# Another token order, merged quarter tiles and an earlier input split in a fused attention and two-mixture kernel on one core

## The chip, the cores and the metric

One Trainium2 chip, one of its cores. The metric is the device time of one execution in microseconds, the median of the runs; the profile is of one further execution, whose own time is given beside its span.

## The reference

Attention with sigmoid weights, then two feed-forward blocks ("mixtures") on its output, all in fp32 at the surface:

```python
# q, k, v: (4, 12, 448, 64)
scores = scale * np.matmul(q, k.transpose(0, 1, 3, 2)) - np.log(S)
attn_out = np.matmul(1.0 / (1.0 + np.exp(-scores)), v)
x = attn_out.transpose(0, 2, 1, 3).reshape(B * S, H * D)       # (1792, 768)
h = x @ w_in;  x = (h * np.cos(h)) @ w_out                     # d_ff 2048
g = x @ w_gate; val = x @ w_val
out = (g * (1.0 / (1.0 + np.exp(-g))) * val) @ w_out2          # d_ff 1536
```

The weights come as 64-bit floats and are converted on the chip.

## The kernel before, in words

**Attention.** 24 pairs of heads, two per round of the loop in `attention` (L759 on). Each pair's q and k are split by VectorE into a rounded upper part and a rest (`split`, L771 and L772); TensorE makes the scores in three chunks of 128 keys from three products of parts (upper x upper, upper x rest, rest x upper; `scores`, L786), ScalarE takes the sigmoid of a chunk for both heads (`sigmoid`, L777), TensorE multiplies with v (`weigh`, L812, and `weigh_rest`, L821), and ScalarE copies the result out of PSUM into R (`leave`, L829). `beside` (L675) lets the planner lay other work between, in rounds that it takes for TWO_PAIRS (10.3) us long.

**Mixtures.** The tokens lie in two halves (h), each of 896 columns, and a unit is one half with two blocks of 128 hidden features; a stage is one mixture on one half. The first mixture has 16 units, 0 to 7 on the first half and 8 to 15 on the second; the second mixture has 12, 16 to 27. An up projection is done by a seven-product scheme (Strassen-Winograd): for each of the products 1 to 7 TensorE runs 9 matmuls of 448 columns (three inner blocks, three products of parts), L1093. The four results are the quarters 11, 12, 21 and 22 of the hidden matrix: the first digit is the feature block (i), the second the column half (j). A down projection of a unit is six down steps, each of 12 matmuls (L995); those of a unit run inside the next one. The order within a unit is a string of tokens (L293 to L296): a digit is an up product, "d" is a down step. `tokens` gives unit 0 and 1 the two strings in FIRST, later units of the first mixture ONE[c % 2] with c the number of the unit before within its stage (so unit 2 has ONE[1], unit 3 has ONE[0], and so on), units of the second mixture TWO twice (for the gate and the value), the last unit the two strings in LAST. Unit c of a stage does the column half j = c % 2 first in its down steps (`down_order`, L305): three steps for one half, then three for the other.

**PSUM.** Up products add in four banks a, b, d, e: 1 goes to a; `first_copy` takes a to b, and 2 adds to b (quarter 11); 6 adds to a; `second_copy` (L1027) takes a to e and 3 adds to e; 7 adds to a, 5 has d. `fifth`, `sum22` and `sum12` form quarters 22 and 12 in SBUF; 4 adds to a and gives 21. A token 2 or 6 waits for the first copy, 7 or 3 for the second, 4 for `sum22`. Down steps have two pairs of banks; `accumulate` (L937) takes a finished pair into R, and `banker` (L963) gives it to a later step, in some cases after a copy of earlier sums into it ("banks<-r").

**The path of a quarter.** In the first mixture `h_cos_h` (L905) does five steps on 448 columns (ScalarE `u`, VectorE `stt`, ScalarE sin, VectorE mult) and then `split_g` (L895): ScalarE rounds the result into the upper part of a g tile, VectorE writes the rest. In the second mixture ScalarE takes silu of the gate quarter and VectorE multiplies with the value's (`silu`, `silu_val`). There are six rooms for 448-column tiles (`tmps`) and four for g (`gslots`); a pair of g rooms comes free after the third and the sixth down step of a unit (L1008), and they go to the first that asked.

**Inputs.** x of a stage is split into upper part and rest for the seven products (`inputs`, L687, 1344 columns each, with subtractions before). The first half's are started when the last head of its second batch has left attention (L831), by `source`. X tiles for 7, 3 and 4 lie in memory that is lent to weight conversions until the end of attention: `lend_pool` (L423) runs four rooms of conversions, ENDS = ((18, 22),) stops new ones at pair 18 and takes the memory back at pair 22 (`swap`).

**Weights.** A converted tile goes back to DRAM and is loaded from there, combined for the scheme (L554), and split into upper part and rest (`operands`, L548; tiles wa, wb, x and s).

**The order of instructions.** Everything besides TensorE's list is ordered at build time by a planner (`Order`, `run` at L155): tasks offer a step with an engine, an assumed duration and a rank; the step that could start first goes next, and among those that could start together the one with the lowest rank. A rank is the time at which the result is due less a number in LEAD (L42), so a larger lead is a higher priority. Each engine then runs its list in that order.

Of the kernel before, what the change touches and what calls it, by code (L numbers as in the profile page):

```python
# [42 lines left out]
    "u": 2.09,  # L43
    "stt": 5.07,
    "sin": 6.46,
    "mult": 5.09,
    "ghi": 0.77,
    "glo": 8.31,
    "whi": 13.87,
    "wlo": 7.59,  # L50
    "c5": -11.35,
    "c7": 2.27,
    "c6": -1.57,
    "c3": -12,
    "xd": 4.42,
    "xhi": 11.87,
    "xlo": -11.87,
    "sv": -0.31,
    "acc": -11.58,
    "bank": -12,  # L60
    "first": -2.82,
    "second": -5.86,
    "fifth": 2.76,
    "s22": 35.5,
    "s12": -3.54,
    "silu": 14.75,
    "conv": 19.14,
    "by abs": 0.0,
    "by sum": 0.0,
    "by x": 0.0,  # L70
# [111 lines left out]
def block_kernel(  # L182
# [29 lines left out]
    def f32(ap):  # L212
        return ap.bitcast(F32)
# [60 lines left out]
    TWO_PAIRS = 10.3  # L274
    ENDS = ((18, 22),)
# [147 lines left out]
    def lend_pool(raw_qk):  # L423
# [9 lines left out]
        def swap():  # L433
            assert all(back.time is not None for back in backs)
# [25 lines left out]
    def conversions(raw=None, t=None, back=None, stop=None):  # L460
# [41 lines left out]
        if not ended:  # L502
            ended.append(True)
            free_t.give(room[:, :WT])
            free_t.give(room[:, WT:])
        else:
            for a in range(3):
                tmps.give(room[:, a * N:(a + 1) * N])
# [175 lines left out]
    source = [order.event() for _ in range(n_stages)]  # L684
    x_open = order.event()

    def inputs(s):  # L687
# [39 lines left out]
        yield source[s]  # L727
# [3 lines left out]
    def attention():  # L731
        with tc.tile_pool(name="at", bufs=2) as at:
# [52 lines left out]

            def scores(i):  # L786
                both = parts.pop(i)
                for c in range(NCH):
                    sc = score[i, c] = score_banks()
                    for n, (m, p) in enumerate(THREE):  # L790
                        for j, half in enumerate(heads):
                            nc.tensor.matmul(  # L792
                                sc[:, j], lhsT=both[half, m, S + c * P:S + (c + 1) * P], rhs=both[half, p, :S],
                                start=n == 0, stop=n == 2,
                            )
                    yield
# [54 lines left out]
            for i in range(0, NPAIR, 2):  # L851
# [25 lines left out]
                for stop, (last, after) in zip(stops, ENDS):  # L877
                    if i == last // 2 * 2:
                        stop[0].append(True)
                    if i == after // 2 * 2:  # L880
                        stop[1]()
            weigh(NPAIR - 1)
# [12 lines left out]
    def split_g(key, f, free):  # L895
        g = yield gslots
        n, _, j = key
        time = due["g", n, j]
        yield by(time - LEAD["ghi"], copy(0.6, g[:, 1], f))
        yield by(time - LEAD["glo"], vec(0.65, g[:, 0], f, f32(g[:, 1]), SUB))  # L900
        gs[key] = g
        g_ready[key].set()
        free()

    def h_cos_h(key, h, read):  # L905

        u = yield tmps
        time = due["g", key[0], key[2]]
        whole = u.bitcast(I32)
        yield by(time - LEAD["u"], act(0.55, out=whole, in_=h, func=AF.Copy, scale=INV2PI, bias=0.25))  # L910
        yield {"DVE": 0.66}, lambda _: nc.vector.scalar_tensor_tensor(
            out=u, in0=h, scalar=INV2PI, in1=whole, op0=ALU.mult, op1=ALU.subtract
        ), time - LEAD["stt"]
        yield by(time - LEAD["sin"], act(0.6, out=u, in_=u, func=AF.Sin, scale=2.0 * math.pi, bias=0.5 * math.pi))
        yield by(time - LEAD["mult"], vec(0.62, u, u, h, ALU.mult))
        read()
        yield from split_g(key, u, lambda: tmps.give(u))

    def silu(z, h, read, done, time):
# [297 lines left out]
```

## Time and profile before

| | us |
|---|---|
| median of 3 runs | 1064.78 (1064.68 to 1065.48) |
| profiled execution, its own time | 1063.94 |
| its span, first to last instruction | 1062.2 |
| TensorE busy (PE) | 1046.7 |
| VectorE busy (DVE) | 844.0 |
| ScalarE busy (ACT) | 628.2 |

The page has PE at 99% of the span, VectorE at 79%, ScalarE at 59%, GpSimd (POOL) at 15%. Times in the rows are us from the span's start unless marked ns. An idle time in brackets is that of the engine just before the row, with what released it. Matmul ends are modelled: one shows 0.36 us, while the next starts 0.2 us after it, so a printed idle time of PE is shorter than the delay of the starts. L258 and L261 are the helpers through which ScalarE's and VectorE's planned steps go, so tiles tell these apart. The first mixture begins at 136.5 us and ends near 575, the last matmul is at 1058.

### The profile page before, as it was taken

How to read it: one execution, taken by the hardware profiler on the slowest of the kernel's cores; microseconds unless marked ns; L12 is line 12 of the kernel's file. 1: busy time of each engine (PE TensorE's matmuls, PEld its weight loads, DVE VectorE, ACT ScalarE, POOL GpSimd, SP SyncE). 2: the span in 40 equal slices, each digit the busy share in tenths (PEclk: the TensorE clock that was granted, in tenths of full speed). 3: DMA queues.
4: the chain of work that ended last, by engine and by line, in shares of the span. 5: the costliest groups of instructions: out<-in, count | busy, mean ns of one | idle time of the engine just before them, and what ended most of it. 6: DMA issues, size and time to landing. Idle time of an engine off the chain costs nothing.

```text
span 1062.2 us, 14669 instructions
## 1 busy us (share of the span) xinstructions
PE 1046.7 (99%) x5459; PEld 914.0 (86%) x5459; DVE 844.0 (79%) x1116; ACT 628.2 (59%) x938; POOL 157.1 (15%) x139
## 2 busy tenths in 40 slices
PE   9999999999999999999999999999999999999998
PEld 4444479998988999999989999999999999999997
DVE  4779869998999988898899898888879744655644
ACT  5777766766778666676677656445444454433430
POOL 2120001112112201111021021111131110110100
PEclk9999999999999999999999999999999999999999
DMA  9997235656563245454422655554422412212002
GB/s 250 305 320 194 92 120 187 204 180 216 195 226 117 74 150 187 155 193 150 149 89 82 217 193 193 204 198 178 143 66 92 156 50 60 75 45 60 30 1 104
DMA packets 63047, 156.68 MB, mean 148 GB/s; under 512 B 9344, under 2 KB 35968, under 8 KB 62976
## 3 DMA queue, kind: packets, MB, share of 16 engines
q1 hardware_dynamic: 60096, 142.11, 41.9%
q0 software_dynamic: 2592, 13.17, 3.6%
q8 instruction: 43, 0.70, 0.3%
q10 hardware_dynamic: 288, 0.46, 0.2%
q14 instruction: 28, 0.23, 0.1%
HBM read 123.47 MB, written 32.24 MB: 147 GB/s over the span
## 4 chain that ended last, share of the span: by engine, by line
PE 89%; DVE 6%; ACT 3%; DMA 1%; issue 1%; SPq 0%; ACTq 0%; DVEq 0%
PE banks L1093 43%; PE banks L995 34%; PE banks L812 5%; PE banks L792 5%; DVE r L261 2%; DVE x L261 1%; PE banks L821 1%; PE banks L803 1%; ACT banks L258 1%; DMA raw<-in_w_in 1%; DVE u L261 0%; ACT x L700 0%; DMA rqk<-in_qk 0%; DVE wa L261 0%; DVE wb L261 0%
## 5 line engine op out<-in xcount | busy, mean ns | idle before, releaser
L1093 PE MATMUL banks<-x,wb 128*128 128x448 f32 x1044 | 224.6, 362 | 3.1 <-ACT banks L258 3.0
L995 PE MATMUL banks<-g,wb 128*128 128x448 f32 x1044 | 224.5, 362 | 0.7 <-DVE wb L261 0.5
L1093 PEld LDWEIGHTS banks<-x,wb 128*128 128x128 f32 x1044 | 195.3, 187 | 18.3 <-ACT banks L258 5.3
L1093 PE MATMUL banks<-x,wa 128*128 128x448 f32 x954 | 206.2, 363 | 3.0 <-ACT banks L258 2.5
L995 PEld LDWEIGHTS banks<-g,wb 128*128 128x128 f32 x1044 | 195.5, 187 | 14.6 <-DVE wb L261 0.9
L1093 PEld LDWEIGHTS banks<-x,wa 128*128 128x128 f32 x954 | 178.2, 187 | 18.3 <-ACT banks L258 4.4
L995 PE MATMUL banks<-g,x 128*128 128x448 f32 x540 | 115.7, 362 | 0.0
L261 DVE TENSOR_TENSOR r<-banks,r 128x896 f32<-128x896 f32 (+1 forms) x69 | 74.0, 1074 | 47.2 <-PE banks L995 46.9
L995 PEld LDWEIGHTS banks<-g,x 128*128 128x128 f32 x540 | 101.2, 187 | 6.8
L258 ACT ACTIVATE u<-u 128x448 f32<-128x448 f32 (+1 forms) x115 | 65.2, 574 | 65.5 <-DVE u L261 56.6
L261 DVE TENSOR_TENSOR u<-u,banks 128x448 f32<-128x448 f32 x117 | 72.0, 616 | 38.7 <-PE banks L1093 37.4
L258 ACT ACTIVATE g<-u 128x448 fp32r<-128x448 f32 x102 | 58.1, 574 | 69.3 <-DVE u L261 56.8
L995 PE MATMUL banks<-g,wa 128*128 128x448 f32 x432 | 92.4, 363 | 2.6 <-ACT banks L258 2.6
L777 ACT ACTIVATE a<-banks 128x896 f32<-128x896 f32 x84 | 75.0, 927 | 33.7 <-PE banks L792 28.7
L995 PEld LDWEIGHTS banks<-g,wa 128*128 128x128 f32 x432 | 80.8, 187 | 9.1 <-ACT banks L258 3.7
L261 DVE TENSOR_TENSOR wb<-t,wb 128x768 fp32r<-128x768 f32 x73 | 72.7, 1000 | 7.9 <-ACT wb L258 7.3
L1093 PE MATMUL banks<-x,s 128*128 128x448 f32 x360 | 78.5, 362 | 0.0
L554 POOL TENSOR_TENSOR sum<-t 128x384 f32<-128x384 f32 x21 | 26.3, 1251 | 339.6 <-DMA t<-swi 136.8
L258 ACT ACTIVATE banks<-banks 128x448 f32<-128x448 f32 x80 | 42.2, 528 | 56.5 <-PE banks L1093 53.8
L261 DVE TENSOR_TENSOR g<-u,g 128x448 fp32r<-128x448 f32 x102 | 66.5, 656 | 10.1 <-ACT g L258 10.1
L1093 PEld LDWEIGHTS banks<-x,s 128*128 128x128 f32 x360 | 67.5, 188 | 4.5
L258 ACT ACTIVATE r<-banks 128x896 f32<-128x896 f32 x52 | 47.6, 918 | 35.8 <-PE banks L995 35.8
(106 smaller groups left out, 1410.8 us busy)
## 6 DMA issues: line engine op xcount, KB each, us to landing
raw<-in_w_out SPq DMA_DIRECT2D x24, 768.0 KB, 4.8
t<-swi SPq DMA_DIRECT2D x32, 384.0 KB, 3.6
t<-swo SPq DMA_DIRECT2D x64, 192.0 KB, 2.9
rqk<-in_qk SPq DMA_DIRECT2D x46, 224.0 KB, 8.2
raw<-in_w_gate SPq DMA_DIRECT2D x12, 768.0 KB, 4.9
raw<-in_w_val SPq DMA_DIRECT2D x12, 768.0 KB, 5.8
t<-swd SPq DMA_DIRECT2D x44, 192.0 KB, 2.5
raw<-in_w_in SPq DMA_DIRECT2D x9, 768.0 KB, 4.7
```

Of the source, the lines that this page charges most:

```text
L258: return {"ACT": time}, lambda _: nc.scalar.activation(**kw)
L261: return {"DVE": time}, lambda _: nc.vector.tensor_tensor(out=out, in0=in0, in1=in1, op=op)
L554: on.tensor_tensor(out=out, in0=a, in1=b, op=op)
L777: nc.scalar.activation(out=a, in_=score.pop(key), func=AF.Sigmoid, bias=-math.log(S), scale=1.0 / math.sqrt(D))
L792: nc.tensor.matmul(sc[:, j], lhsT=both[half, m, S + c * P:S + (c + 1) * P], rhs=both[half, p, :S], start=n == 0, stop=n == 2,)
L803: nc.tensor.matmul(sc[rows, j], lhsT=raw[half, 1, REST:], rhs=raw[half, 0], start=True, stop=True)
L812: nc.tensor.matmul(banks[half, 6 + i % 2, :S], lhsT=vw[:, c, j], rhs=a[:, j], start=c == 0, stop=False, skip_group_check=True,)
L821: nc.tensor.matmul(banks[half, 6 + odd, :S], lhsT=last_v[rows, i // 2 % (2 * NS), j], rhs=a[rows, j], start=False, stop=True, skip_group_c ...
L995: nc.tensor.matmul(banks[:, first + e - d, :N], lhsT=w[:, m, e % KH, :], rhs=g[:, 1 - p], start=(i, m, p) == (0, 0, 0) and is_fresh and no ...
L1093: nc.tensor.matmul(bank, lhsT=w[:, m, k, :], rhs=x[p][:, k], start=(k, m, p) == (0, 0, 0) and i in (1, 5), stop=(k, m) == (KH - 1, 1), ski ...
```

## The change

Five things, cut to what matters:

- **Tokens.** FIRST[1], ONE[0] and LAST[1] are other strings with the same tokens.
- **First scores.** For the first pair of heads the upper x upper products of all three chunks are issued ahead of the other products.
- **Inputs of the first mixture.** Each of the seven x tiles waits for the quarter of R that it is made of (one batch, three head pairs), not for both batches. The lent rooms are taken back at pair 20 or, where their conversions are not through, at a later one. TWO_PAIRS is 10.9.
- **Two quarters as one tile.** `tmps` has three rooms of 2 x 448 columns and `gslots` two; quarters 12 and 22 go through `h_cos_h`, `silu`, `silu_val` and `split_g` as one tile of 896 columns after `sum12`, while 11 and 21 share a room and are handled one by one. A raw room that is given over at the end of the conversions yields one such tile instead of three single ones.
- **Leads.** Nearly all numbers in LEAD; three of them change assumed durations ("by abs" -0.26, "by sum" -0.08, "by x" +0.28: what the planner adds to VectorE's time for the absolute value of a weight, a weight sum, a cast of x).

```diff
-    "u": 2.09,      "stt": 5.07,    "sin": 6.46,    "mult": 5.09,   "ghi": 0.77,
-    "glo": 8.31,    "whi": 13.87,   "wlo": 7.59,    "xd": 4.42,     "xhi": 11.87,
-    "acc": -11.58,  "bank": -12,    "first": -2.82, "second": -5.86, "fifth": 2.76,
-    "by abs": 0.0,  "by sum": 0.0,  "by x": 0.0,
+    "u": -2.16,     "stt": 6.03,    "sin": 38.7,    "mult": 6.36,   "ghi": -11.5,
+    "glo": 5.57,    "whi": 11.53,   "wlo": 17.79,   "xd": -7.79,    "xhi": 8.43,
+    "acc": -9.4,    "bank": -7.95,  "first": -11.16, "second": 16.47, "fifth": 27.3,
+    "by abs": -0.26, "by sum": -0.08, "by x": 0.28,
...
-    TWO_PAIRS = 10.3
-    ENDS = ((18, 22),)
+    TWO_PAIRS = 10.9
+    ENDS = ((18, 20),)
...
-    FIRST = ('1652734', '1562d7d3dd4dd')
-    ONE = ('15267ddd3d4dd', '15d2d6d7d3d4d')
+    FIRST = ('1652734', '156d273ddd4dd')
+    ONE = ('1526d7dd3d4dd', '15d2d6d7d3d4d')
-    LAST = ('1526d734', '15d6273dddd4')
+    LAST = ('1526d734', '1d652d7d3dd4')
...
+            if s < NH:
+                yield left_attention[h, wanted[i]]
...
-        yield source[s]
+        wanted = {1: (0, 0), 2: (0, 1), 5: (1, 0), 7: (1, 1), 6: (1, 1), 4: (0, 1), 3: (1, 1)}
+        if s >= NH:
+            yield source[s]
...
+                for c in range(NCH if i == 0 else 0):
+                    product(both, banks[:, 2 * c:2 * c + 2, :S], c, 0)
                 for c in range(NCH):
                     sc = score[i, c] = score_banks()
+                    for n in range(1 if i == 0 else 0, 3):
+                        product(both, sc, c, n)
...
+                order.now = max(order.now, TWO_PAIRS * (i // 2 + 1) + 12.5)
-                if b % 2 and k == NP - 1:
-                    source[b // 2].set()
+                if k % KH == KH - 1:
+                    left_attention[b // 2, (b % 2, k // KH)].set()
...
-    def split_g(key, f, free):
-        g = yield gslots
+    def split_g(n, j, i, f, free):
+        both = i is None
+        if both:
+            g = yield gslots
+            halves["g", n, j] = [g, order.event(), 2]
+            part = g
+        else:
+            part = yield from half("g", (n, i, j), gslots)
+        hi, lo = (part[:, :, 1], part[:, :, 0]) if both else (part[:, 1], part[:, 0])
...
         def fifth():
-            keep["12"] = yield tmps
-            keep["22"] = yield tmps
+            two = keep["two"] = yield tmps
+            keep["12"], keep["22"] = two[:, 0], two[:, 1]
...
         def sum12():
-            yield from after("12", keep["12"], lambda: None)
+            two = keep["two"]
+            if layer == 1:
+                order.spawn(h_cos_h(n, 1, None, two, lambda: tmps.give(two)), 3)
...
-            for i in range(4):
-                gslots.give(mp.tile([P, 2, N], F32R, tag=f"g{i}", name=f"g{i}"))
-            for i in range(5):
-                tmps.give(mp.tile([P, N], F32, tag=f"u{i}", name=f"u{i}"))
+            for i in range(2):
+                gslots.give(mp.tile([P, 2, 2, N], F32R, tag=f"g{i}", name=f"g{i}"))
+            for i in range(2):
+                tmps.give(mp.tile([P, 2, N], F32, tag=f"u{i}", name=f"u{i}"))
```

## Rows read from the trace of the kernel before

**Rows 1.** The page's busy line of TensorE and its chain by engine.
```profile
PE 1046.7 (99%) x5459; PEld 914.0 (86%) x5459; DVE 844.0 (79%) x1116; ACT 628.2 (59%) x938; POOL 157.1 (15%) x139
...
PE 89%; DVE 6%; ACT 3%; DMA 1%; issue 1%; SPq 0%; ACTq 0%; DVEq 0%
```
**Rows 2.** Busy time by stretch: length, PE, PEld, DVE, ACT, POOL, clock, DMA.
```profile
260.00:360.00 100.00, 96.54 (x476) 88.46 (x476) 95.84 (x125) 76.89 (x115) 16.37 (x12) 1.00 0.51 172
...
562.80:790.00 227.20, 227.08 (x1134) 212.51 (x1135) 191.60 (x260) 121.78 (x186) 39.14 (x30) 1.00 0.51 170
```
**Rows 3.** Who waited for whom, PE alone: total us, times, longest.
```profile
PE banks L1093 <- ACT banks L258: 5.5, 9, 0.8
```
**Rows 4.** Timeline of PE in unit 3 (ONE[0]): start, length, work, idle before.
```profile
210.72 1.96 PE L1093 MATMUL banks<-x,x 128*128 128x448 f32 x9
213.30 2.08 PE L1093 MATMUL banks<-x,wb 128*128 128x448 f32 x9 [0.62 <-ACT banks L258]
```
**Rows 5.** Timeline of ScalarE at the same place.
```profile
212.72 0.53 ACT L258 ACTIVATE banks<-banks 128x448 f32<-128x448 f32 x1 [0.52 <-PE banks L1093]
```
**Rows 6.** Timelines of PE and VectorE in unit 5 (ONE[0]).
```profile
269.22 2.08 PE L1093 MATMUL banks<-x,wa 128*128 128x448 f32 x9 [0.62 <-ACT banks L258]
...
269.01 0.62 DVE L261 TENSOR_TENSOR g<-u,g 128x448 fp32r<-128x448 f32 x1
```
**Rows 7.** Timeline of PE at the first scores.
```profile
6.10 0.74 PE L792 MATMUL banks<-qk 64*128 64x448 f32 x2 [0.65 <-DVE qk L771]
7.16 5.17 PE L792 MATMUL banks<-qk 64*128 64x448 f32 x34 [0.32 <-DVE qk L772]
```
**Rows 8.** Groups by form: count, then busy us, mean ns, idle before.
```profile
L261 DVE TENSOR_TENSOR r<-banks,r 128x896 f32<-128x896 f32 x67 | 72.8, 1087 | 46.5 <-PE banks L995 46.3
...
L258 ACT ACTIVATE r<-banks 128x896 f32<-128x896 f32 x52 | 47.6, 918 | 35.8 <-PE banks L995 35.8
L258 ACT ACTIVATE u<-u 128x448 f32<-128x448 f32 x83 | 47.3, 574 | 47.3 <-DVE u L261 38.6 <-DVE u L911 8.5
...
L261 DVE TENSOR_TENSOR u<-u,u 128x448 f32<-128x448 f32 x48 | 30.4, 634 | 0.5 <-ACT u L258 0.4
```
**Rows 9.** Timelines of PE, ScalarE, VectorE: unit 4's start, then the tail.
```profile
233.21 1.96 PE L1093 MATMUL banks<-x,wb 128*128 128x448 f32 x9
...
234.90 0.62 DVE L261 TENSOR_TENSOR g<-u,g 128x448 fp32r<-128x448 f32 x1
...
236.31 0.62 DVE L261 TENSOR_TENSOR g<-u,g 128x448 fp32r<-128x448 f32 x1
...
1041.74 0.58 ACT L258 ACTIVATE g<-raw 128x448 fp32r<-128x448 f32 x1 [5.55 <-PE banks L995]
...
1042.35 0.62 DVE L261 TENSOR_TENSOR g<-raw,g 128x448 fp32r<-128x448 f32 x1 [3.72 <-ACT g L258]
...
1043.94 3.76 PE L995 MATMUL banks<-g,wb 128*128 128x448 f32 x18
```
**Rows 10.** Busy time of VectorE by stretch in attention: length, busy, clock, DMA.
```profile
20.00:40.00 20.00, 11.87 (x18) 1.00 1.06 296
...
80.00:100.00 20.00, 19.86 (x21) 1.00 0.70 185
```
**Rows 11.** Timeline of PE at other waits of the first mixture.
```profile
258.72 1.48 PE L995 MATMUL banks<-g,wa 128*128 128x448 f32 x6 [0.74 <-ACT banks L258]
...
298.52 0.68 PE L995 MATMUL banks<-g,wb 128*128 128x448 f32 x2 [0.22 <-ACT wb L258]
299.72 1.07 PE L995 MATMUL banks<-g,wb 128*128 128x448 f32 x4 [0.52 <-DVE wb L261]
...
344.85 1.48 PE L995 MATMUL banks<-g,wa 128*128 128x448 f32 x6 [1.48 <-ACT banks L258]
```
**Rows 12.** ScalarE in attention (timeline), then its casts of x (groups).
```profile
18.68 0.92 ACT L777 ACTIVATE a<-banks 128x896 f32<-128x896 f32 x1 [0.40 <-PE banks L812]
...
L700 ACT ACTIVATE x<-r 128x1344 fp32r<-128x1344 f32 x20 | 26.5, 1324 | 10.7 <-PE banks L1093 6.2 <-DVE r L261 4.4
```

More of the change, by code (lines that the diff above doesn't have):

```diff
@@ L42 @@
 LEAD = {
[L43 to L66, printed above, removed]
+    "u": -2.16,
+    "stt": 6.03,
+    "sin": 38.7,
+    "mult": 6.36,
+    "ghi": -11.5,
+    "glo": 5.57,
+    "whi": 11.53,
+    "wlo": 17.79,
+    "c5": -11.17,
+    "c7": -1.62,
+    "c6": -12,
+    "c3": -2.55,
+    "xd": -7.79,
+    "xhi": 8.43,
+    "xlo": -12,
+    "sv": 6.71,
+    "acc": -9.4,
+    "bank": -7.95,
+    "first": -11.16,
+    "second": 16.47,
+    "fifth": 27.3,
+    "s22": 17.01,
+    "s12": 2.09,
+    "silu": 40.74,
     "conv": 19.14,
-    "by abs": 0.0,
-    "by sum": 0.0,
-    "by x": 0.0,
+    "by abs": -0.26,
+    "by sum": -0.08,
+    "by x": 0.28,
 }
@@ L433, in swap @@
         def swap():
-            assert all(back.time is not None for back in backs)
+            if any(back.time is None for back in backs):
+                return
+            backs.append(order.event())
             pool.__exit__(None, None, None)
@@ L506, in conversions @@
         else:
-            for a in range(3):
-                tmps.give(room[:, a * N:(a + 1) * N])
+            tmps.give(room[:, :2 * N].rearrange("p (i t) -> p i t", i=2))
     def landed(event, t=None):
@@ L879, in attention @@
                         stop[0].append(True)
[L880 removed]
+                    if i >= after // 2 * 2:
                         stop[1]()
+            assert x_open.time is not None
             weigh(NPAIR - 1)
@@ L893, in block_kernel @@
     gs = {}
-    def split_g(key, f, free):
-        g = yield gslots
-        n, _, j = key
-        time = due["g", n, j]
[L899 to L902, printed above, removed]
-        free()
[L905 to L911, printed above, removed]
+    halves = {}
@@ new lines, in half, with give_half @@
+    def half(kind, key, slots):
+        n, i, j = key
+        if (kind, n, j) not in halves:
+            halves[kind, n, j] = [None, order.event(), 2]
+            halves[kind, n, j][0] = yield slots
+            halves[kind, n, j][1].set()
+        yield halves[kind, n, j][1]
+        return halves[kind, n, j][0][:, i]
+    def give_half(kind, key, slots):
+        n, _, j = key
+        entry = halves[kind, n, j]
+        entry[2] -= 1
+        if not entry[2]:
+            slots.give(halves.pop((kind, n, j))[0])
@@ new lines, in split_g @@
+    def split_g(n, j, i, f, free):
[7 more added lines that the diff above has]
+        hi, lo = (part[:, :, 1], part[:, :, 0]) if both else (part[:, 1], part[:, 0])
+        time = due["g", n, j]
+        yield by(time - LEAD["ghi"], copy(0.92 if both else 0.6, hi, f))
+        yield by(time - LEAD["glo"], vec(1.1 if both else 0.65, lo, f, f32(hi), SUB))
+        for e in range(2) if both else (i,):
+            gs[n, e, j] = g[:, e] if both else part
+            g_ready[n, e, j].set()
+        free()
@@ L912, in h_cos_h @@
+    def h_cos_h(n, j, i, h, read):
+        both = i is None
+        u = (yield tmps) if both else (yield from half("u", (n, i, j), tmps))
+        time = due["g", n, j]
+        whole, wide = u.bitcast(I32), 0.37 if both else 0.0
+        yield by(time - LEAD["u"], act(0.55 + wide, out=whole, in_=h, func=AF.Copy, scale=INV2PI, bias=0.25))
+        yield {"DVE": 0.66 + 1.3 * wide}, lambda _: nc.vector.scalar_tensor_tensor(
             out=u, in0=h, scalar=INV2PI, in1=whole, op0=ALU.mult, op1=ALU.subtract
@@ L919, in silu, with silu_val @@
-    def silu(z, h, read, done, time):
-        yield by(time, act(0.6, out=z, in_=h, func=AF.Silu))
+        yield from split_g(n, j, i, u, lambda: tmps.give(u) if both else give_half("u", (n, i, j), tmps))
+    def silu(z, h, read, done, time, wide=0.0):
+        yield by(time, act(0.6 + wide, out=z, in_=h, func=AF.Silu))
         read()
         done.set()
-    def silu_val(key, z, z_done, h, read, free, time):
+    def silu_val(n, j, i, z, z_done, h, read, free, time):
         yield z_done
-        yield by(min(time, due["g", key[0], key[2]] - LEAD["sv"]), vec(0.62, z, z, h, ALU.mult))
+        yield by(min(time, due["g", n, j] - LEAD["sv"]), vec(0.62 if i is not None else 1.1, z, z, h, ALU.mult))
```

60 lines of the change are left out of this document (33 added, 27 removed).

## Prediction

> **What bounds the kernel now.** I read the page's busy line and its chain first. TensorE is busy 1046.7 us and carries 89% of the chain that ended last [rows 1]. The kernel ends when TensorE has gone through its list, so time is won only where TensorE stands still; the reader should look for gaps on PE. The table by stretch says where they lie: 3.46 us of 100 in 260 to 360 us, 0.12 of 227.2 in 562.8 to 790 us [rows 2]. The second mixture hardly waits, the first does. The list of PE's waits says for what: 5.5 us in 9 waits of up products (L1093) for a ScalarE copy that reads and writes PSUM [rows 3].
>
> The PE timeline shows what one such wait costs. The up product at 210.72 has 9 matmuls 0.2 us apart, so the next could begin at 212.52. It begins at 213.30: 0.78 us, and about 0.11 more while the pipeline fills again: 0.89 us are lost where the row prints an idle time of 0.62 [rows 4]. So I add 0.27 to a printed idle time. The copy that it waits for starts at 212.72, when the product has drained, and lasts 0.53 us [rows 5]. This is token 7 right behind token 6: `second_copy` must take bank a to bank e before 7 adds to a.
>
> **The change part by part.**
>
> *Token order.* ONE[0] has "67" side by side before and "6d7" after. Units 3, 5, 7, 9, 11, 13 and 15 run ONE[0], so there are seven such waits; the row at 213.30 stands for them. A down step is 12 matmuls, 2.4 us, against a copy of 0.53 us and hand-offs of about 0.2: well covered. Removed: 7 x 0.89 = **6.2 us**. What is late next is the down step that is pulled ahead: it starts 0.89 + 1.8 = 2.7 us sooner and needs its half's g tiles by then. In the unit whose token 7 started at 269.22 VectorE wrote one g tile from 269.01 for 0.62 us, until 269.63 [rows 6]; the down step came 1.91 us after token 7's start and would now start 2.7 us before that, at 268.4. So 1.2 us are short in that unit if the order stays. The list is made anew with the nearer due time and this g tile stood behind work that is due later, so I take 0; bounds 0 and 1.2, and rival (b) is the case in which it is the rule.
>
> *The first scores.* TensorE does two matmuls at 6.10 and then waits for the lower part of the split until 7.16 [rows 7]. With the first product of all three chunks ahead, six matmuls stand in this hole. The 34 that follow take 5.17 us [rows 7], 0.30 us for the two of a pair of heads. Two pairs move: 0.6 us at most, 0 if the sigmoids set the pace. I take **0.5 us**, nearer the upper end, since TensorE's row starts on its own split and no sigmoid becomes later.
>
> *Two quarters as one tile.* An ACTIVATE of 448 columns lasts 574 ns, one of 896 lasts 918; VectorE's tensor_tensor 634 and 1087 ns [rows 8]. Merging two saves 230 ns on ScalarE and 180 ns on VectorE; a unit of the first mixture has three of each, 0.7 and 0.5 us of 27. VectorE is busy 95.84 of 100 us in 260 to 360 us [rows 2], so this is relief where it is short, but not on TensorE's path: it counts under the waits below.
>
> *What the merged tile costs.* The second pair's room for g is free only when the last down step of the unit before is through. The conversion is then one ScalarE pass of 0.92 and one VectorE pass of 1.09 us [rows 8], both ahead of the first matmul; with hand-offs, 2.2 to 2.3 us. Two places have little room.
> At the end LAST[1] now has "3dd4": one up product, 1.8 us, stands between that down step and the first of the closing six. Before, this late conversion starts at 1041.74 and ends at 1042.97, and the closing six start unhindered at 1043.94 [rows 9]. Merged, it starts when the step has drained, 1042.3, and ends near 1044.4: **+0.6 us** with the refill; bounds 0.3 and 0.9.
> In the units with an odd number the next one starts with "15d", 3.6 us of room, seven places (units 1 to 13). In the one that began at 233.21, behind unit 3, VectorE ended the two late conversions at 235.52 and 236.93 [rows 9], 2.3 and 3.7 us after. A single pass needs about 1.4 of that, so the first one queued 0.9 us. A merged one with this queueing is through at 3.2 of 3.6 us. I take 0.15 each, **+1.0 us**; bounds 0 and, with the second one's queueing of 2.3 us, 1.1 each, 7.7 us.
>
> The Trainium skill, Perfetto Trace Analysis, section Optimizing Scalar/DVE Operations, speaks against merging here: where these two engines are not saturated but hold up another, breaking instructions up may end the work sooner. VectorE's rows at the tail are idle for the most part, so by that rule single tiles would leave the 0.6 us out and the sum would be 1056.4; no run here shows both forms.
>
> *Inputs split as their heads leave, rooms given back, TWO_PAIRS.* Before, the first stage's x tiles wait for the last head of the second batch, and VectorE is then full, 19.86 of 20 us in 80 to 100 us, while it had 11.87 of 20 in 20 to 40 us [rows 10]. What moves is casts and subtractions into that idle time, and what it frees is time for two to four more weight conversions in attention. Cover: TensorE's own work in attention hides both engines. If it fails by the planner's longer round (10.9 against 10.3 us), a full VectorE slips by at most 0.2 us in each of some nine rounds, 2 us; a ScalarE that gets the casts is rival (c). I take 0, since VectorE's idle time in 20 to 40 us is the nearest row.
>
> *The other waits of the first mixture.* The largest are at 258.72, 298.52, 299.72 and 344.85 [rows 11]: with 0.27 each, 1.01 + 0.49 + 0.79 + 1.75 = 4.0 us. The two near 299 wait for weights that ScalarE and VectorE split late; with earlier conversions and less VectorE work they go: -1.3. The other two wait for a down bank that `banker` fills with earlier sums, behind the same full engines; the new leads reorder them, and between all gone and as much again (-2.8 to +2.8) I take half gone, by the relief above: -1.4. Together **-2.7 us**.
>
> **Sum.** The profiled run's own time is 1063.94 us: its span of 1062.2 and 1.74 around it. The median of the runs, 1064.78, is 0.84 above; the sum is put on the median. -6.2 - 0.5 + 0.6 + 1.0 - 2.7 = -7.8: **1057.0 us**.
>
> **The rivals.**
> (a) *Only the token order counts.* The other waits move but stay: -6.2 - 0.5 + 0.6 + 1.0 = -5.1, **1059.7 us**. For it: a lead decides only among steps that are ready at the same time. Against: VectorE gets less work in a stretch that is 96% full.
> (b) *The wait moves.* The down step waits for g where 7 waited for its copy, so the 6.2 us stay: -0.5 + 0.6 + 1.0 - 2.7 = -1.6, **1063.2 us**. For it: 269.63 against 268.4 [rows 6]. Against: that needs 0.9 us in all seven units, and VectorE only has to take that one pass earlier.
> (c) *Slower: casts of x on ScalarE among the sigmoids.* The lead "by x" makes the planner count a cast on VectorE 0.28 us dearer, and a longer round leaves a start on ScalarE open in it. A cast lasts 1.32 us there; between sigmoids ScalarE had idle times of 0.40 us [rows 12], and TensorE waits for sigmoids in each half round. It decides from a cast that is queued ahead of a sigmoid in a gap shorter than 1.32 us. Seven casts that hide nothing cost 9.2 us: -5.1 + 9.2 = +4.1, **1068.9 us** with the other waits staying. For it: the four hand-over gaps are short. Against: the q/k scores run ahead by three chunks, and before the change VectorE took these casts.
> (d) *The room for g comes too late* in all seven units, 7.7 in place of 1.0: -2.7 other waits kept: -7.8 + 6.7 = -1.1, **1063.7 us**. Against: the 2.3 us of queueing belong to a second pass behind a first, and the merged tile has only one.
> That the first scores gain nothing is 0.5 us on any of these.
>
> **How the numbers follow.** Forecast 0.50 (1053 to 1058.3); (a) 0.27 (1058.3 to 1062); (b) below its full price 0.06 (1062 to 1062.6), so faster 0.83; (b) and (d) near their price, 0.09, are within 0.2%, which is about what a measurement of this kernel can tell from no change (2.1 us); (c) and its like 0.08, slower. Low end: all four other waits gone, first scores at 0.6, no new wait but the tail's 0.6: -6.2 - 0.6 - 4.0 + 0.6 = -10.2, 1054.6; the two waits that the list counts beside the seven [rows 3] (5.5 - 7 x 0.62 = 1.2 us printed, 1.7 with 0.27 each) may give up to 2 more: 1052.5. High end 1062.5, which leaves (b), (d) and (c) out, 0.17.
>
> **What would show it.** Right: tokens 6, d, 7 without a gap and PE's waits on L1093 for ScalarE copies down from 9 to about 2; no PE gap near 6.8 us; ScalarE and VectorE rows of u and g with 896 columns; x tiles from about 30 us on; more loads of `lr` than before; a gap of half a microsecond ahead of the last 72 matmuls. Wrong: PE waiting for g ahead of the first down step of a unit; new waits in attention; the waits for weights near 299 us still there, which would mean that the earlier x split bought no conversion.

## The result: 0.84% faster

| | us | before, beside it | ratio, 95% interval |
|---|---|---|---|
| before | 1064.78 | | |
| after | 1055.61 (1053.94 to 1058.6, 4 runs) | 1064.73 | 0.9916 [0.989, 0.9942] |
| after, profiled execution | 1054.24, span 1052.4 | 1063.94, span 1062.2 | |

The forecast was 1057.0 in a range of 1052.5 to 1062.5. The profiled executions differ by 9.7 us, in their own times as in their spans. Where that came from can be counted on TensorE. From the first up product on I added up by how much each matmul starts later than 0.2 us after the one before it; this is called **lost** below. The time from the first score to the first up product is called the length of **attention**. The end is counted from 0.2 us behind the start of the last matmul.

| us | before | after | difference |
|---|---|---|---|
| lost in the mixtures | 14.65 | 4.12 | -10.53 |
| attention | 130.38 | 131.34 | +0.96 |
| from the last matmul to the end | 3.82 | 3.69 | -0.13 |
| sum | | | -9.70 |

So the mixtures gave more than the whole, and attention took a tenth of it back.

The page of after, its busy line and its chain by engine, beside [rows 1]; then the table by stretch, beside [rows 2]:

```profile
PE 1043.5 (99%) x5459; PEld 914.9 (87%) x5459; DVE 839.9 (80%) x1049; ACT 618.3 (59%) x866; POOL 154.7 (15%) x140
...
PE 95%; DMA 2%; POOL 1%; DVE 1%; ACT 0%; issue 0%; POOLq 0%; ACTq 0%; DVEq 0%; SPq 0%
```
```profile
260.00:360.00 100.00, 100.00 (x502) 93.75 (x501) 91.96 (x108) 72.44 (x101) 21.01 (x15) 1.00 0.42 138
```

In that stretch TensorE's idle 3.46 us are gone and VectorE is busy 4 us less. Who waited for whom, PE alone, whole span (total us, times, longest), beside [rows 3]:

```profile
PE banks L815 <- ACT a L783: 1.5, 2, 0.9
...
PE banks L1038 <- DVE r L261: 1.0, 1, 1.0
PE banks L1141 <- ACT banks L258: 0.7, 1, 0.7
...
PE banks L1038 <- DVE g L261: 0.2, 1, 0.2
```

Of the nine waits of up products (L1141, before L1093) for a ScalarE copy one is left. It stands in unit 0 in both kernels. The largest wait is new and lies in attention: L815, scores that wait for a sigmoid. (Before, the list has one wait of TensorE for a sigmoid, of 0.2 us.) The place of [rows 4 and 5] in unit 3, PE and then ScalarE:

```profile
210.95 1.96 PE L1141 MATMUL banks<-x,x 128*128 128x448 f32 x9
212.75 2.56 PE L1038 MATMUL banks<-g,wa 128*128 128x448 f32 x12
215.15 1.96 PE L1141 MATMUL banks<-x,wb 128*128 128x448 f32 x9
...
212.95 0.53 ACT L258 ACTIVATE banks<-banks 128x448 f32<-128x448 f32 x1 [0.72 <-PE banks L1141]
```

Token 6, the down step and token 7 follow each other to the hundredth (1.8 and 2.4 us), and the copy, 212.95 to 213.48, lies under the down step.

### The profile page after: what moved, and what is told of

It is laid out like the page before. It is cut to its first block, busy times and chain, and to the rows that moved or that the text cites. A ratio compares the mean times of both kernels' runs of the same rounds, so it can differ in the third digit from the quotient of the medians.

```text
span 1052.4 us, 14528 instructions
## 1 busy us (share of the span) xinstructions
PE 1043.5 (99%) x5459; PEld 914.9 (87%) x5459; DVE 839.9 (80%) x1049; ACT 618.3 (59%) x866; POOL 154.7 (15%) x140
## 4 chain that ended last, share of the span: by engine, by line
PE 95%; DMA 2%; POOL 1%; DVE 1%; ACT 0%; issue 0%; POOLq 0%; ACTq 0%; DVEq 0%; SPq 0%
PE banks L1141 47%; PE banks L1038 38%; PE banks L824 5%; PE banks L795 4%; DMA vs<-in_v 1%; PE banks L815 1%; PE banks L833 1%; DMA t<-swi 1%; POOL cv L555 1%; DMA rqk<-in_qk 0%; DVE wa L261 0%; ACT g L258 0%; DVE r L261 0%; POOL sum L555 0%; DVE g L261 0%
## 5 line engine op out<-in xcount | busy, mean ns | idle before, releaser
L1141 PE MATMUL banks<-x,wb 128*128 128x448 f32 x1044 | 224.1, 362 | 0.0
L1141 PEld LDWEIGHTS banks<-x,wb 128*128 128x128 f32 x1044 | 195.8, 188 | 13.0
L1141 PE MATMUL banks<-x,wa 128*128 128x448 f32 x954 | 205.8, 362 | 0.9 <-ACT banks L258 0.7
L1141 PEld LDWEIGHTS banks<-x,wa 128*128 128x128 f32 x954 | 178.6, 187 | 14.6 <-ACT banks L258 1.5
L261 DVE TENSOR_TENSOR u<-u,banks 128x448 f32<-128x448 f32 x124 | 76.2, 616 | 62.2 <-PE banks L1141 60.0
L258 ACT ACTIVATE wb<-t 128x768 fp32r<-128x768 f32 x75 | 62.9, 838 | 50.5 <-PE banks L1141 34.0
L555 POOL TENSOR_TENSOR sum<-t 128x384 f32<-128x384 f32 x26 | 35.3, 1358 | 344.5 <-DMA t<-swi 121.3
L1141 PE MATMUL banks<-x,s 128*128 128x448 f32 x360 | 78.5, 362 | 0.0
L261 DVE TENSOR_TENSOR g<-u,g 128x448 fp32r<-128x448 f32 (+1 forms) x78 | 68.8, 890 | 11.4 <-ACT g L258 11.1
L258 ACT ACTIVATE wa<-t 128x768 fp32r<-128x768 f32 x61 | 51.0, 840 | 40.8 <-PE banks L1141 18.0
L258 ACT ACTIVATE g<-u 128x448 fp32r<-128x448 f32 (+1 forms) x78 | 54.0, 699 | 35.4 <-PE banks L1038 18.8
```

The costliest lines, as they stand in the source:

```text
L258: return {"ACT": time}, lambda _: nc.scalar.activation(**kw)
L261: return {"DVE": time}, lambda _: nc.vector.tensor_tensor(out=out, in0=in0, in1=in1, op=op)
L555: on.tensor_tensor(out=out, in0=a, in1=b, op=op)
L1141: nc.tensor.matmul(bank, lhsT=w[:, m, k, :], rhs=x[p][:, k], start=(k, m, p) == (0, 0, 0) and i in (1, 5), stop=(k, m) == (KH - 1, 1), ski ...
```

## The experiments

Each kernel was timed, and profiled once; its ratio is to runs of the kernel before beside it, whose medians were 1064.47 to 1065.59 us. "Lost" and attention are those of the one profiled execution.

| | edit | us (low to high) | ratio to before | lost in mixtures | attention | `lr` loads |
|---|---|---|---|---|---|---|
| before | | 1064.78 | | 14.65 | 130.38 | 11 |
| after | | 1055.61 (1053.94 to 1058.6) | 0.9916 [0.989, 0.9942] | 4.12 | 131.34 | 14 |
| e1 | before with the new ONE[0] | 1080.97 (1079.95 to 1085.59) | 1.0151 [1.012, 1.0182] | 28.77 | 132.31 | 11 |
| e2 | after with the old ONE[0] | 1063.74 (1061.56 to 1066.26) | 0.9978 [0.9965, 0.999] | 12.36 | 130.82 | 14 |
| e3 | after with the old input split | 1076.65 (1073.01 to 1079.73) | 1.0095 [1.0066, 1.0124] | 19.70 | 138.44 | 12 |
| e4 | after with the old first scores | 1053.52 (1053.24 to 1053.96) | 0.988 [0.9863, 0.9897] | 4.04 | 130.51 | 14 |
| e5 | after, unchanged | 1054.38 (1053.02 to 1054.97) | 0.9889 [0.987, 0.9908] | 4.16 | 130.18 | 14 |
| e6 | after with single tiles | 1063.42 (1061.0 to 1066.93) | 0.9978 [0.9964, 0.9992] | 11.76 | 133.86 | 14 |
| e7 | after with the old leads | 1064.8 (1063.47 to 1068.87) | 0.9999 [0.9983, 1.0014] | 14.92 | 130.25 | 14 |
| e8 | after, landings assumed later | 1059.59 (1059.09 to 1061.26) | 0.9942 [0.9923, 0.996] | 4.05 | 136.24 | 14 |
| e9 | after, loads from 78 us on | 1055.23 (1054.3 to 1056.08) | 0.9902 [0.9882, 0.9921] | 4.07 | 131.61 | 14 |
| e10 | after, leads rounded | 1055.24 (1054.38 to 1056.13) | 0.9899 [0.9877, 0.9921] | 4.07 | 133.16 | 14 |
| e11 | before, leads rounded | 1068.91 (1066.74 to 1071.91) | 1.0031 [1.0015, 1.0047] | 17.82 | 132.36 | 11 |
| e12 | e8 and e9 together | 1053.25 (1052.73 to 1053.61) | 0.9895 [0.9879, 0.9912] | 4.09 | 130.20 | 14 |

Two of the sums hold a second thing besides waits: 4.4 us of e1's 28.77 and 1.6 us of e7's 14.92 were lost by matmuls that ran at a lower clock behind a wait. That is told below.

### The token string, alone and taken back (e1, e2)

```diff
-    ONE = ('15267ddd3d4dd', '15d2d6d7d3d4d')
+    ONE = ('1526d7dd3d4dd', '15d2d6d7d3d4d')
```

> The kernel before with one string changed: ONE[0] is '1526d7dd3d4dd'. Theory (the token order hides the copy): the seven waits of 0.89 us ahead of token 7 go, 6.2 us, time 1058.5 us; PE's waits of L1093 for ScalarE copies fall from 9 to 2. Rival (the wait moves): the down step that is pulled ahead waits for its g tile, PE's waits for g or for weights grow by as much, time 1063 to 1065 us.

e2 is this diff turned round, in the kernel after.

> The changed kernel with ONE[0] as before. Theory: seven waits of 0.89 us come back, 6.2 us more, 1061.8 us. Rival (in the new schedule other things bound the first mixture): less than 3 us more, under 1058.5 us.

In e1 the seven waits of token 7 are gone, as the step says, and the kernel is 1.5% **slower**, far outside both the theory and its rival. Four lines of PE's waits in e1, then two places of its timeline, in unit 5's down step and in unit 8, and the table by stretch right behind the second:

```profile
PE banks L1093 <- DVE x L261: 4.7, 2, 3.6
PE banks L995 <- ACT banks L258: 3.3, 2, 2.3
PE banks L1093 <- DVE u L261: 3.1, 2, 2.7
PE banks L995 <- ACT wb L258: 2.9, 2, 1.5
...
303.77 0.67 PE L995 MATMUL banks<-g,wb 128*128 128x448 f32 x2 [1.50 <-ACT wb L258]
...
363.75 2.61 PE L1093 MATMUL banks<-x,wb 128*128 128x448 f32 x6 [3.59 <-DVE x L261]
...
363.39:366.80 3.41, 3.04 (x8) 2.75 (x9) 3.41 (x4) 0.00 (x0) 1.42 (x1) 0.50 0.56 190
```

TensorE now waits for weights, x tiles, bank copies and quarters that the two other engines made in time before. VectorE is busy 96 of 100 us in the first mixture [rows 2], and with another string the planner makes another list throughout: 6.4 us went and 20.6 came. Of the 20.6, waits are 16.2. The other 4.4 were lost behind them: in three stretches (305.36 to 308.78, 363.39 to 366.80 and 820.78 to 824.19 us) the granted clock of TensorE was 0.50, the lower of its two levels (1.2 of 2.4 GHz), and matmuls started 0.37 us apart in place of 0.20. In each case TensorE had stood still shortly before, for 1.50 and 1.31, 3.59, and 2.70 us. In e2 the same seven waits come back with the old string:

```profile
PE banks L1141 <- ACT banks L258: 5.2, 8, 0.8
```

(eight with the one in unit 0), and 8.24 us are lost more than in after. So the string ONE[0] decides those seven waits in either kernel, but what it is worth depends on what it stands beside: -8.2 us lost in the mixtures from e2 to after, +14.1 from before to e1. Which steps of e1's list made each of its waits was not followed.

### The earlier input split (e3)

```diff
-    TWO_PAIRS = 10.9
-    ENDS = ((18, 20),)
+    TWO_PAIRS = 10.3
+    ENDS = ((18, 22),)
...
-            if s < NH:
-                yield left_attention[h, wanted[i]]
...
+        yield source[s]
...
-                if k % KH == KH - 1:
-                    left_attention[b // 2, (b % 2, k // KH)].set()
+                if b % 2 and k == NP - 1:
+                    source[b // 2].set()
```

> The changed kernel with the first inputs split only after both batches have left, rooms taken back at pair 22 and TWO_PAIRS 10.3 as before; tokens, merging, leads and first scores stay. Theory (the earlier split buys conversions in attention, and these remove the waits for weights): the loads of lr fall back from 14 to about 11, waits for weights of 1.3 to 2.8 us come back between 250 and 350 us, and the two waits of 1.8 us in attention go: 1055 to 1057 us. Rival (merging and leads alone relieve the first mixture): no wait comes back there, attention loses its 1.8 us: 1053 to 1054 us.

This is the dearest part to take back: 1076.65 us, some 20 us above what either side expected. The edit takes back several things at once: the split by quarters, the late return of the rooms, TWO_PAIRS, and the line that moves `order.now` on in `leave`. Two places of PE's timeline in e3, one in attention and one in unit 5's down step:

```profile
72.46 3.26 PE L817 MATMUL banks<-a,vs 128*64 128x448 f32 x8 [6.27 <-DMA vs<-in_v]
...
308.99 0.66 PE L1029 MATMUL banks<-g,wb 128*128 128x448 f32 x2 [1.49 <-ACT wb L258]
310.78 1.08 PE L1029 MATMUL banks<-g,wb 128*128 128x448 f32 x4 [1.13 <-DVE wb L261]
```

The down step is that of [rows 11] near 299 us, in unit 5, which stands still for weights. With it goes the number of weight conversions that fit into attention, read from the DMA issues of `lr` in after:

```profile
lr<-in_w_in POOLq DMA_DIRECT2D x8, 768.0 KB, 9.7
...
lr<-in_w_out POOLq DMA_DIRECT2D x6, 768.0 KB, 10.3
```

14 here, 7 + 4 = 11 before. Over all kernels: wherever 11 or 12 were loaded, that down step waits (before 1.29 us, e1 3.92, e3 3.17, e11 1.33); wherever 14 were, it doesn't (after, e2, e4 to e10, e12). That the earlier split buys conversions, and that these free unit 5, rests on this. The wait in attention is another matter. In e3's chain it is a load of v:

```profile
58.42 13.90 DMA vs<-in_v
```

Behind it the granted clock was 0.50 from 70.83 to 77.65 us, and the weighing at 72.46 took 4.68 us where the next one took 2.40. Which part of the edit let this load become late was not followed.

### The first scores (e4), and the spread of the kernel after (e5)

```diff
-                for c in range(NCH if i == 0 else 0):
-                    product(both, banks[:, 2 * c:2 * c + 2, :S], c, 0)
...
-                    for n in range(1 if i == 0 else 0, 3):
-                        product(both, sc, c, n)
+                    for n, (m, p) in enumerate(THREE):
```

> The changed kernel with the first pair's scores in the old order. Theory: 0.6 us more ahead of the first weighing, kept until the end. Rival (the sigmoids set the pace behind the first scores): no difference in the start of the first weighing or in the time.

e5 is the kernel after once more.

> The changed kernel itself, beside the others of this call. Theory (two waits in attention depend on when loads land, and the first scores' lead shifts them): 1054 to 1058 us, runs further apart than those of the kernel with the first scores in the old order (1053.2 to 1054.0). Rival (the 2 us between the two came from the chip): 1053.5 us here too.

From the first score to the first weighing it is 7.08 us before, 7.13 in e4 and 7.11 in e11 with the old order; 6.60 in after, 6.60 in e8, 6.59 in e10 and 6.59 in e12 with the new one: 0.5 us are won. In all of these executions the pairs of first scores start 0.37 us apart until about 10 us, and 0.20 after that. That is the clock again, as the table by stretch of e9 shows, whose pairs are 0.20 apart until 7.6 us, then 0.37 apart until 11 us:

```profile
4.14:7.55 3.41, 1.88 (x12) 0.96 (x12) 1.62 (x2) 0.00 (x0) 0.00 (x0) 1.00 1.08 210
7.55:10.97 3.42, 3.42 (x22) 2.92 (x22) 1.62 (x2) 2.68 (x4) 1.08 (x2) 0.50 1.08 249
```

Where the pairs start 0.20 us apart from the first one on, the new order wins nothing that can be seen: 6.25 us in e1, which has the old order, against 6.12 to 6.73 in e2, e3, e5, e6 and e7, which have the new one. There TensorE waits for VectorE's split of the next pair either way, 0.30 us in e1 and 0.49 in e5.

The 0.5 us don't reach the end: e4 isn't slower than after or e5, the intervals overlap. What eats them are the waits for sigmoids. From the first weighing to the first up product, less the printed waits for sigmoids, it is 123.2 us in e4, after and e10 and 123.3 in e5; the waits themselves are 0.2, 1.5, 3.4 and 0.4 us.

### Two quarters as single tiles again (e6), the old leads (e7)

```diff
-            tmps.give(room[:, :2 * N].rearrange("p (i t) -> p i t", i=2))
+            for a in range(3):
+                tmps.give(room[:, a * N:(a + 1) * N])
...
-        yield by(time - LEAD["ghi"], copy(0.92 if both else 0.6, hi, f))
-        yield by(time - LEAD["glo"], vec(1.1 if both else 0.65, lo, f, f32(hi), SUB))
+        yield by(time - LEAD["ghi"], copy(0.6, g[:, 1], f))
+        yield by(time - LEAD["glo"], vec(0.65, g[:, 0], f, f32(g[:, 1]), SUB))
```

> The changed kernel with single tiles for quarters 12 and 22 as before, everything else changed. Theory (merging relieves VectorE in the first mixture and the leads are made for it): its tail wait of 0.45 us goes, but waits for weights and g come back, 3 to 8 us more, 1058 to 1063 us. Rival (merging is off the path): 1055 us, within 1 us of the changed kernel.

In e7 the leads are those of before; the three "by" durations stay new.

```diff
-    "u": -2.16,
-    "stt": 6.03,
-    "sin": 38.7,
...
+    "u": 2.09,
+    "stt": 5.07,
+    "sin": 6.46,
```

> The changed kernel with the leads of before; only the three assumed durations stay changed. Theory (the strings decide which waits are possible, the leads whether they happen, as the kernel with the one string alone shows): 10 to 25 us more, 1065 to 1080 us, as waits of a microsecond or more all over the first mixture. Rival (my prediction's view that a lead only chooses among ready steps and is worth the 2.7 us of the other waits): 1058 to 1060 us.

Either of them alone takes back 7.6 to 10.8 us in the mixtures, e7 all that the change brought (ratio 0.9999), just short of what its theory expected. What comes back in both is the wait of down steps for a bank that is filled with earlier sums, which [rows 11] show at 258.72 and 344.85; in after 0.30 us are lost to it, at one place (554.59). PE's waits of e6, then of e7:

```profile
PE banks L1010 <- ACT banks L258: 3.8, 3, 2.0
```
```profile
PE banks L1038 <- ACT banks L258: 6.1, 5, 2.1
```

In e6 they stand in units 6 and 12 (2.27 and 1.65 us lost), in e7 in units 6, 10, 12 and 14 (1.05, 1.69, 1.69, 3.97; 1.6 of the last were lost at a granted clock of 0.50, from 560.65 to 564.06). In 260 to 360 us VectorE is busy 93.90 us in e6 and 91.96 in after. e6 has no wait at the tail, after has one. The rest of e6's loss is smaller waits, most of them for weights, and its attention is 2.5 us longer than after's, with 4.0 us of waits for sigmoids.

### The new waits in attention (e8, e9, e12)

The 1.5 us for sigmoids in after's list of waits are two places, 0.61 us at 33.80 and 0.93 at 56.19. The second one's rows in after, PE, ScalarE and GpSimd, with the load from the chain of waits; last the step on ScalarE behind which the first one's sigmoid stood:

```profile
56.19 0.98 PE L815 MATMUL banks<-rqk 64*64 64x448 f32 x8 [0.93 <-ACT a L783]
...
54.80 0.53 ACT L258 ACTIVATE s<-sum 128x384 fp32r<-128x384 f32 x1 [0.61 <-POOL sum L555]
55.24 0.90 ACT L783 ACTIVATE a<-banks 128x896 f32<-128x896 f32 x1
...
53.56 1.22 POOL L555 TENSOR_TENSOR sum<-t 128x384 f32<-128x384 f32 x1 [4.39 <-DMA t<-swi]
...
45.62 7.80 DMA t<-swi
...
32.04 0.91 ACT L258 ACTIVATE lr<-lr 128x768 int32<-128x768 uint32 x1 [1.43 <-DMA lr<-in_w_in]
```

Read from the load on: it takes 7.80 us where the planner assumes 5.0; GpSimd's sum waits for it, ScalarE's rounding of the sum waits for GpSimd, and the sigmoid stands behind that rounding in ScalarE's list; it has no idle time of its own ahead, so its place in the list is what held it. At the first place it is an `lr` load, for which ScalarE stood 1.43 us. e8 lets the planner assume 9.0 us in attention:

```diff
-            yield LANDING
+            yield LANDING + (4.0 if order.now < 100.0 else 0.0)
```

> The changed kernel with one assumption of the planner changed: in attention a load of weights lands 4 us later than it took so far (9 in place of 5 us; the trace has 7.8 us for the one ahead of the wait at 56 us). Theory: the weight split that stands ahead of a sigmoid goes behind it, the wait of 1.0 us at 56 us goes, and the runs lie closer together: 1053.5 to 1055 us. Rival (a replanned list brings new waits of a few us, as with the one string alone): 1058 us or more.

That theory fell: attention got 4.9 us longer. The load went to 53.22 and took still longer, and ScalarE stood behind it all the same (e8, chain of waits, GpSimd, ScalarE, PE, table by stretch):

```profile
53.22 12.48 DMA t<-swi
...
65.84 0.98 POOL L555 TENSOR_TENSOR sum<-t 128x384 f32<-128x384 f32 x1 [9.49 <-DMA t<-swi]
...
66.86 0.52 ACT L258 ACTIVATE s<-sum 128x384 fp32r<-128x384 f32 x1 [5.01 <-POOL sum L555]
...
69.03 1.77 PE L815 MATMUL banks<-rqk 64*64 64x448 f32 x8 [3.77 <-ACT a L783]
...
67.91:74.74 6.83, 5.71 (x20) 1.55 (x20) 5.67 (x6) 5.20 (x8) 3.23 (x4) 0.50 0.96 274
```

The wait of 3.77 us is 2.2 more than after's two together. The clock cost another 2.8: the 20 matmuls from 69.03 on took 6.08 us, nearly all at a granted clock of 0.50, where after's from 56.19 on took 3.32.

e9 keeps these loads out of the first 78 us:

```diff
+        yield 78.0
```

> The changed kernel with the first loads of converted weights held back to 78 us, when q, k and v have stopped filling the DMA engines; nothing else is edited. Theory (attention's new waits are sigmoids queued on ScalarE behind a weight split whose load lands late): PE's waits for sigmoids at 33 to 57 us shrink to those of a late lr load (0.3 us or less), attention shortens by about 1 us against the changed kernel's 130.2 to 131.4, time 1053 us. Rival (any such edit makes a new list, and waits of a few us appear in the first mixture): lost time after 137 us of 8 us or more in place of 4.1, 1058 us or more.

Attention got no shorter than after's: the wait of the sums is gone, and one of 1.54 us stands at 88.59 in its place, again behind a load on ScalarE (e9, ScalarE):

```profile
86.09 0.85 ACT L258 ACTIVATE wa<-t 128x768 fp32r<-128x768 f32 x1 [2.06 <-DMA t<-swi]
```

e12 has both edits.

> The changed kernel with loads of converted weights held back to 78 us, and with 4 us more assumed for their landing in attention (the load at 82.48 us of the kernel that only held them back was issued 4 us later than its list supposed). Theory (a weight split queued on ScalarE ahead of a sigmoid and waiting for a load is what attention loses): no wait for a sigmoid over 0.4 us, attention at 129.5 to 130 us from the first score to the first up product, 4.1 us lost after that as before, the first scores' 0.5 us kept, 1052.5 to 1053.5 us. Rival (another load, of q, k, v or a raw weight, sets the pace there anyway): waits of a microsecond elsewhere in attention, 1054 to 1056 us.

One wait for a sigmoid is left in attention, 0.5 us, and attention took 130.20, both a little more than expected:

```profile
PE banks L816 <- ACT a L784: 0.5, 1, 0.5
```

e12's runs lie within 0.9 us of each other (1052.73 to 1053.61), those of after's list within 4.7, 2.0 and 1.8 (after, e5, e10). Its ratio of 0.9895 [0.9879, 0.9912] overlaps with after's: that it is faster is not shown, only that these few runs lie closer.

### Leads without their hundredths (e10, e11)

All leads rounded to whole numbers, in after (e10) and in before (e11), for instance in e10

```diff
-    "stt": 6.03,
-    "sin": 38.7,
+    "stt": 6,
+    "sin": 39,
```

> The changed kernel with every lead rounded to a whole number, a change of half a microsecond at most. Theory (strings, merging and earlier inputs hold the gain; a lead only has to have the right size): lost time in the mixtures stays within 1 us of 4.1 us, 1054 to 1056 us. Rival (this one list fits, a close neighbour does not): 4 us more or worse, 1058 to 1066 us.

> The kernel before with every lead rounded to a whole number. By the theory that a lead only has to have the right size: 1064 to 1066 us. By the rival (the list of before was such a fit too): 1068 us or more, lost time in the mixtures of 18 us or more in place of 14.7.

e10's lists are after's, engine by engine, so it is a third profile of one list, and its times are after's too. It can't tell whether a close neighbour of the list would do as well. Its attention took 133.16 us, with 3.4 us of waits for sigmoids where e5 has 0.4 (e10's waits, then its chain of waits, then after's chain):

```profile
PE banks L815 <- ACT a L783: 3.4, 2, 2.1
...
32.65 14.34 DMA vs<-in_v
...
47.06 8.42 DMA t<-swi
...
31.83 13.72 DMA vs<-in_v
...
45.62 7.80 DMA t<-swi
```

The load that holds up the second sigmoid took nearly the same time in the three profiles of the list, 8.19 us in e5, 7.80 in after and 8.42 in e10. What differs is when it was issued: at 43.81, 45.62 and 47.06, each time 0.07 us behind the landing of a load of v that took 12.47, 13.72 and 14.34 us. So one late load holds back the next one's issue, and that one a sigmoid. The executions of e5 and e10 were on different chips, so the chip may have a part in it; the four times of after alone lie 4.7 us apart.

In e11 changes of at most half a microsecond in the leads were enough for another list: 3.2 us lost more, and a wait of 2.0 us for v in attention.

```profile
PE banks L1093 <- ACT banks L258: 6.5, 9, 1.3
PE banks L812 <- DMA vs<-in_v: 2.0, 1, 2.0
```

## Why the prediction was right, and where it wasn't

**Bound.** Right: TensorE's own work is the same, and the time went where TensorE stood still, most of it in the first mixture.

**Token order, -6.2.** Right in size: the seven waits cost 6.45 us lost in before and nothing in after, 0.92 each where 0.89 was put. Nothing came in their place: of rival (b) the list of waits has one for g in 28 units, and it is the one at the tail. What was wrong is that the step stood by itself. Taken alone the string costs 1.5% (e1). The sentence "the list is made anew with the nearer due time" set this at 0, bounds 0 and 1.2; e1 has 16.2 us of new waits, for other things than g, and 4.4 us at the lower clock behind them. Beside the other parts the string pays (e2). That it needs them all is not shown; that taking back the leads, the merging or the early inputs costs more than its 6.4 us is (e7, e6, e3).

**First scores, -0.5.** Right at its place, 0.5 us, where the first scores ran at the lower clock, as in the rows that it was read from: their 0.30 us per pair [rows 7] is a mean of 0.37 and 0.20. It is worth nothing that can be measured at the end (e4). The step that failed is the cover that was taken for the rest of attention: its end is set by loads and by ScalarE's list behind them, too, and these move it by 3 us between executions of one list.

**Merged tile at the tail, +0.6.** Measured 0.44. After's PE, with VectorE's pass between:

```profile
1032.10 1.96 PE L1141 MATMUL banks<-x,wb 128*128 128x448 f32 x9
...
1033.28 1.09 DVE L261 TENSOR_TENSOR g<-raw,g 128x896 fp32r<-128x896 f32 x1 [4.04 <-ACT g L258]
```

The up product ends its starts at 1033.90 and the pass ends at 1034.37; VectorE had been idle for 4.04 us before it, as foreseen. The wait is in every kernel that merges and in none of those that don't (before, e1, e6, e11). The Trainium skill, Perfetto Trace Analysis, section Optimizing Scalar/DVE Operations, has it that where these two engines are not saturated but hold up another, breaking instructions up may let work end sooner. At the tail the trace agrees, by 0.44 us. The first mixture is not such a place, with VectorE busy 93.90 of 100 us in e6; over the whole kernel e6 goes the other way, 7.6 us lost more with single tiles.

**Merged tile in the odd units, +1.0.** Too dear: 0.25 us at one place, in the down step at 506.15. The queueing of 0.9 us that the step carried over from unit 3's rows [rows 9] did not recur. With it rival (d) falls.

**Early split, 0.** As a sum right only by luck: it is not an edit that costs and brings nothing, but the one without which the rest is slower than before (e3, 1.0095, with all of its parts taken back at once). The prediction had its use, two to four conversions more (three came), and its sign at the waits near 299 us, where it booked 1.3 of the sum's gain. What it did not have are the new waits in attention, 1.5 us in the profiled execution, which it named as a sign of being wrong. That the early split brought them is not shown: after has them, e4 with the same split has 0.2, and e12 0.5.

**Other waits, -2.7.** Right in kind, too small: all that is left besides, 7.25 us before, is 2.47 after, -4.78. The two waits for weights went, as booked (1.57 us lost with their neighbours). The two waits for a bank went altogether (2.78), where half was taken; this is the term that was mis-sized, by 1.4 us. Waits of this kind come back when either the merged tile or the leads are taken back (e6, e7). And smaller ones went with them, a further 0.4 net: the one wait that is new, 1.26 us lost at 809.98 in the second mixture, stands against those.

Against the measured -9.7 the sum of -7.8 so missed by -1.4 in the bank waits, -0.75 in the odd units, -0.4 in the smaller waits and -0.7 in the token order, the weight waits and the tail together; attention went the other way, +0.96 where the first scores' -0.5 was booked, +1.5, nearly all of it waits for sigmoids. (The stretch after the last matmul makes up the last -0.1.)

**Rivals.** (a) put the time at 1059.7 because a lead would decide only among steps that are ready together. Whether it does or not, that is enough to move everything: the old leads alone take the whole gain back (e7). (c) was right that ScalarE holds up sigmoids with other work ahead of them, and wrong about the work: it is a conversion that waits for a load, 0.4 to 3.4 us in all. Its premise that TensorE waits for sigmoids in each half round does not stand in the trace of before, which has one such wait, of 0.2 us. Its casts did come, two of the seven on ScalarE (70.48 and 81.53) and five on VectorE, and TensorE did not wait behind these two. Below are ScalarE's first cast with the sigmoids after it, TensorE's rows around it, and the first cast on VectorE, all in after:

```profile
70.48 1.34 ACT L702 ACTIVATE x<-r 128x1344 fp32r<-128x1344 f32 x1 [0.44 <-DVE r L261]
71.72 2.52 ACT L783 ACTIVATE a<-banks 128x896 f32<-128x896 f32 x3
...
70.18 2.09 PE L795 MATMUL banks<-qk 64*128 64x448 f32 x18
72.20 2.48 PE L824 MATMUL banks<-a,vs 128*64 128x448 f32 x12
...
34.22 1.55 DVE L704 CAST x<-r 128x1344 fp32r<-128x1344 f32 x1
```

**Open.** Which of the leads carry the gain, which of e1's steps brought its waits, which part of e3's edit its loss hangs on, what the strings FIRST[1] and LAST[1] do by themselves, and why the loads of v took longer in one execution of a list than in another.

## What to carry to other kernels

The length of a gap is not what closing it is worth when all other lists are planned anew with it: here four parts were each worth -7.6 to -15.6 us lost in the mixtures beside the others, and one of them alone +14. Where engines run lists in order, look at every step that waits for a load and ask what stands behind it on its engine; the cost comes with the time at which the load lands, so it shows as a spread between runs before it shows in a median. Before a difference of half a microsecond is believed, profile the same list twice, and look at the granted clock of the stretch, too: a wait can cost more than its own length.

## What was not expected of the hardware

A load's landing time in attention is no constant. The DMA engines are full there; after's row of 40 to 60 us in the table by stretch has a share of 1.05 and 313 GB/s:

```profile
40.00:60.00 20.00, 19.07 (x136) 8.87 (x134) 18.97 (x22) 16.03 (x22) 7.63 (x8) 1.00 1.05 313
```

There `t<-swi`, 384 KB, which lands in 3.5 us by the median of after's 32, took 7.80 us at 45.62, and 12.48 in e8 when it was issued 7.6 us later. The trace of before already had this: 7.08 us at 39.72 and 11.23 at 54.25. One and the same list had 130.18, 131.34 and 133.16 us of attention in three profiles (e5, after, e10), while the time lost in its mixtures was 4.16, 4.12 and 4.07.

TensorE's granted clock fell to 0.50 during or right behind a wait in four of the profiled executions: e1 (three stretches), e3 (70.83 to 77.65 us, a wait of 6.27), e7 (560.65 to 564.06, one of 2.13) and e8 (67.91 to 74.74, one of 3.77). Matmuls of 448 columns then started 0.37 us apart in place of 0.20. e6 kept its clock through a wait of 3.3 us in attention, so the length of one wait does not settle it. The profiled executions of before and after have no such stretch between their first scores and the last matmul, so the 9.7 us between them are not made by it.
